# Scatter matmuls of hops 2 to 7 as four 32-column matrices instead of one of 128 columns

## The chip, the cores and the metric

The kernel runs on one core of one Trainium2 chip. The metric is the device time of one execution, in microseconds (us), as the median of several runs; lower is better. Beside the runs there is one profiled execution, whose trace gives every instruction's start and length on each engine: PE (TensorE, matmuls; PEld are its weight loads), DVE (VectorE), ACT (ScalarE), POOL (GpSimd) and SP (SyncE, which here only issues DMAs). Ends of matmuls in that trace are modelled.

## What is computed

A graph of N = 10,000 nodes with E = 160,000 random edges and D = 128 features per node. First seven propagations ("hops") of the normalized sum over neighbours, each from the result of the one before; then a small attention over the eight tokens of each node, and a readout.

```python
h = x
toks = [x]
for _ in range(7):
    msg = h[src] * deg_inv_sqrt[src, None] * deg_inv_sqrt[dst, None]
    h = _segment_sum(msg, dst, N)
    toks.append(h)
tok = jnp.stack(toks, axis=1)                      # (N, 8, D)
t = _layernorm(tok, axis=-1)
q, key, v = (einsum('nkd,de->nke', t, w) for w in (wq, wk, wv))
attn = _softmax(einsum('nkd,nld->nkl', q, key) / D ** 0.5, axis=-1)
o = tok + einsum('nkd,de->nke', einsum('nkl,nld->nkd', attn, v), wo)
alpha = _softmax(einsum('nkd,d->nk', _layernorm(o, axis=-1), w_r), axis=-1)
out = einsum('nk,nkd->nd', alpha, o)
```

## The kernel before

**Stages.** The edges are sorted into cells and turned into 0/1 matrices in fp8 (`pass_a`, `decode`, `place`, `matrices`); hop 1 runs between that work, block by block as the matrices appear. The matrices of each block of 128 target nodes are stored in DRAM (`GSd`). Hops 2 to 7 load them again and do nothing else but propagate. The attention follows. The diff touches `block`, which serves hop 1 (`first=True`) and hops 2 to 7 alike.

**A block.** The nodes stand in 79 tiles of 128. The table `tab` holds all node features in SBUF as f16 pairs (a high and a low part, 256 columns per tile). One call of `block` makes one tile of 128 targets:

- *Gather* (`gather(jj)`, L580). For each of NG = 18 groups, four 0/1 matrices of 128 x 32 pick 32 rows each out of four different table tiles. The four matmuls write the partitions 0 to 31, 32 to 63, 64 to 95 and 96 to 127 of the PSUM tile `p`. A call of `gather` makes two groups (eight matmuls), so a block calls it nine times, jj = 0 to 8. `p` rotates over 6 PSUM buffers in hops 2 to 7.
- *Evacuation* (L585, L587). The 128 x 512 result goes to an f16 buffer `e` in SBUF (14 of them in rotation): in hops 2 to 7 ACT takes jj = 0, 2, 4, 5, 7 and DVE jj = 1, 3, 6, 8. A gather that reuses a buffer of `p` waits for its evacuation six gathers earlier.
- *Scatter* (`scat(e, jj)`, L556). For each of the 18 groups one 0/1 matrix of 128 x 128 adds the 128 gathered rows into the 128 targets: a matmul of 256 columns into the PSUM accumulator `acc`, which all 18 share.
- *Rows that didn't fit* (`fetched`, L542). NI + 1 = 2 further groups per block are fetched from DRAM by POOL's indirect DMAs (`fetch`, L526, into `og`) and scattered the same way, with the matrices `w[:, NG * 128:]` and `Sov`. `begin` does so ahead of the scatters; in the first two blocks of a hop (`late`) the second of them comes in `close` (L569).
- *Close* (`close`, L571). DVE adds the high and low halves into `s`; then `entries` writes the new table entries (ACT L616, DVE L617, L618) and `token_out` the token (POOL L625, and a DMA by SP).

**Order.** Hops 2 to 7 run six times over 79 blocks. Within a block PE has all 72 gather matmuls first, then the two fetched groups, then 18 scatters. The scatters lag: `pend` holds closures, and a block leaves the last two of its own scatter calls and its `close` to the next block (`lag` = 2). So a block's 18 scatters are the last four of the block before, and fourteen of its own. POOL's queue has per block: a copy of one column of `e` of jj = 0 (L525, it holds the fetch back until that evacuation is done), the fetch from `tabh` (L526), the fetch from `tabd` (L526), and L625. SP's queue has the load of the next `w` (L752) and the stores.

Each matmul is two PE instructions, a weight load and the matmul. The names to follow: `fetched`, `scat` and `close` in `block` (L530 to L611), `gather` for comparison, and the caller in `run` (L750 to L762).

Of the kernel before, what the change touches and what calls it, by code (L numbers as in the profile page):

```python
# [20 lines left out]
NG = 18  # L21
NI = 1
# [17 lines left out]
class Hops:  # L40
# [169 lines left out]
    def times(self, out, oh, f):  # L210

        self.nc.vector.tensor_tensor(out, oh, f[:, :, None, :].to_broadcast(list(oh.shape)), op=ALU.mult)  # L212
# [317 lines left out]
    def block(self, t, w, tab, og, pend, lag, runs, first, evac, fin, lead=False, late=False, mid=None, ahead=None,  # L530
              after=None):

        nc, V, A, T, G = self.nc, self.nc.vector, self.nc.scalar, self.nc.tensor, self.nc.gpsimd
        m = 257 if first else 256
        acc = []


        def fetched(i, start=False, stop=False):  # L540
            W = w[:, (NG + i) * 128:(NG + i + 1) * 128] if i < NI else self.Sov[:, t, :]
            T.matmul(acc[0][:, :256], W, og[i], start=start, stop=stop)  # L542
            if first:
                T.matmul(acc[0][:, 256:257], W, self.ones16, start=False, stop=False)

        def begin():
            acc.append(self.pacc.tile([128, 512], F32, name="acc", tag="acc"))
            for i in range(NI if late else NI + 1):
                fetched(i, start=i == 0)

        def scat(e, jj):
            if not acc:
                acc.append(self.pacc.tile([128, 512], F32, name="acc", tag="acc"))
            for j in range(e.shape[1]):
                J = 2 * jj + j
                T.matmul(acc[0][:, :m], w[:, J * 128:(J + 1) * 128], e[:, j, :m], start=first and J == 0,  # L556
                         stop=J == NG - 1 and not (first or late))
                if first and J == 0 and not lead:
                    for i in range(NI):
                        fetched(i)  # L560

        def close():
            if first:
                if lead:
                    for i in range(NI):
                        fetched(i)
                T.matmul(acc[0][:, 256:257], self.Sov[:, t, :], self.ones16, start=False, stop=False)
            if first or late:
                T.matmul(acc[0][:, :256], self.Sov[:, t, :], og[NI], start=False, stop=True)  # L569
            s = self.fp.tile([128, 128], F32, name="s")  # L570
            V.tensor_reduce(s, acc[0][:, 0:256].rearrange("p (h d) -> p d h", h=2), axis=X, op=ALU.add)  # L571
            fin(t, s, acc[0])

        def gather(jj):
            n = min(2, NG - 2 * jj)
            p = self.pg.tile([128, 2, 2, 128], F32, name="p")
            for j in range(n):
                for q in range(4):
                    s = 4 * (2 * jj + j) + q
                    T.matmul(p[32 * q:32 * q + 32, j], w[:, NJ * 128 + s * CAP:NJ * 128 + (s + 1) * CAP], tab[:, s, :], start=True, stop=True)  # L580
            e = self.ebuf[self.eb_i % len(self.ebuf)]
            self.eb_i += 1
            pv = p[:, :n].rearrange("p j h d -> p j (h d)")
            if evac(jj):
                A.copy(e[:, :n, 0:256], pv)  # L585
            else:
                V.tensor_tensor(e[:, :n, 0:256], pv, self.one[:, :, None].to_broadcast([128, n, 256]), op=ALU.mult)  # L587
            pend.append(lambda: scat(e[:, :n], jj))

        jj = 0  # L590
        for i, n in enumerate(runs):
            for _ in range(n):
                gather(jj)
                if jj == 0 and not first and not mid:
                    ahead(self.ebuf[(self.eb_i - 1) % len(self.ebuf)][:, 0, 0:1])
                jj += 1
            if mid:
                mid(0)
            if not first:
                begin()  # L600
                if mid:
                    ahead()
            while len(pend) > lag:
                pend.pop(0)()
            if mid:
                mid(1)
            if after:
                after()
            if i == len(runs) - 1:
                pend.append(close)  # L610
            yield  # L611
# [686 lines left out]
```

## Time and profile before

| what | value |
|---|---|
| median of 3 runs | 3991.8 us (3988.98 to 3993.97) |
| the profiled execution | 3999.62 us, span 3997.8 us, mean TensorE clock 0.973 |
| PE busy | 3745.5 us (94%), 69,690 matmuls |
| PEld busy | 3031.4 us (76%) |
| DVE busy | 3322.9 us (83%) |
| ACT busy | 2724.5 us (68%) |
| POOL busy | 1766.6 us (44%) |
| chain that ended last | PE 71%, DVE 19%, ACT 4% |

Hops 2 to 7 take the stretch from about 1192 us to 3300 us of the span; the attention follows it.

How to read the lines: a group's line has the kernel's line, the engine, the operation, the tile written and the tiles read, the shape, the count, then busy time in us, the mean length of one in ns, and the idle time before them with what ended it. `128*32` on a PE line is the shape of the weights: rows by columns. A line of the timeline has start, length, engine, line and operation, merged where equal instructions follow each other (`x18`), and in brackets the idle time before and its inferred releaser; "issue" means that the profile shows nothing that was waited for. A line of the windows has the stretch, its length, busy time with the number of instructions of PE, PEld, DVE, ACT and POOL, then the granted clock of PE, the busy share of the DMA engines and GB/s.

### The profile page before, as it was taken

Reading aid. Unit: us, or ns where it says so; the run is one execution under the profiler, and the core shown is the slowest. Engines: PE = TensorE matmul, PEld = TensorE weight load, DVE = VectorE, ACT = ScalarE, POOL = GpSimd, SP = SyncE. Lnnn points to the kernel's source line nnn. Section 1 sums busy time; section 2 is a strip of 40 time slices with the busy share of each in tenths; the row PEclk is TensorE's granted clock in tenths of the full one; section 3 lists DMA queues with packets and bytes.
Section 4 is the critical chain, followed back from the end, with each engine's and each line's share of the span. In section 5 each row is a group of like instructions: output and inputs, shape, how many; then the busy total and the mean of one; then the engine's idle time right before and its main releaser. Section 6 shows DMA issues by size and latency. Waiting matters only on the chain.

```text
span 3997.8 us, 165094 instructions
## 1 busy us (share of the span) xinstructions
PE 3745.5 (94%) x69690; PEld 3031.4 (76%) x69690; DVE 3322.9 (83%) x6961; ACT 2724.5 (68%) x6830; POOL 1766.6 (44%) x2342
## 2 busy tenths in 40 slices
PE   6886799999989999999999999999999999999997
PEld 4665566666658888888888788878878887788885
DVE  8998999999977777777777777777766666999998
ACT  6884456666666666666666666666665658888884
POOL 0000333333335665666666566656656662222222
PEclk8998899999999999999999999999999999999998
DMA  3100445454556666666666666666656552222220
GB/s 104 32 2 1 134 151 154 149 162 143 156 168 189 201 201 193 202 203 200 193 202 202 185 202 202 202 189 198 202 184 205 186 183 77 74 74 76 78 78 13
DMA packets 321189, 594.93 MB, mean 149 GB/s; under 512 B 56183, under 2 KB 214101, under 8 KB 315189
## 3 DMA queue, kind: packets, MB, share of 16 engines
q1 hardware_dynamic: 282485, 506.62, 40.0%
q0 software_dynamic: 35392, 72.55, 6.3%
q8 instruction: 546, 8.95, 0.9%
q10 hardware_dynamic: 2560, 5.12, 0.4%
q14 instruction: 206, 1.69, 0.1%
HBM read 455.43 MB, written 128.67 MB: 146 GB/s over the span
## 4 chain that ended last, share of the span: by engine, by line
PE 71%; DVE 19%; ACT 4%; issue 2%; DMA 2%; POOL 0%; another core or an unknown queue 0%; SPq 0%; DVEq 0%; ACTq 0%; POOLq 0%
PE p L580 26%; PE acc L556 24%; PE acc L542 4%; DVE w L514 3%; PE pv L972 3%; PE po L983 3%; PE pu L961 3%; DVE ux L219 2%; DVE o L212 2%; ACT rs L340 2%; PE tb L440 2%; PE pt L951 1%; DVE oh L206 1%; DVE R L212 1%; DVE w L511 1%
## 5 line engine op out<-in xcount | busy, mean ns | idle before, releaser
L585 ACT CAST eb<-p 128x512 f16<-128x512 f32 x3065 | 1623.7, 596 | 645.4 <-PE p L580 404.3
L587 DVE TENSOR_TENSOR eb<-p,one 128x512 f16<-128x512 f32 x1912 | 1230.6, 685 | 332.2 <-PE acc L556 195.9
L580 PE MATMUL p<-tab,w 128*32 128x256 f16 x39816 | 1288.7, 274 | 44.2 <-issue 21.4
L556 PE MATMUL acc<-eb,w 128*128 128x256 f16 (+1 forms) x9954 | 1246.9, 274 | 8.4 <-DVE indeg L649 3.1
L580 PEld LDWEIGHTS <-w 128*32 128x32 fp8e4 x39816 | 1002.3, 96 | 261.3 <-issue 225.8
L556 PEld LDWEIGHTS <-w 128*128 128x128 fp8e4 x9954 | 954.3, 98 | 170.3 <-issue 54.9
L526 POOL DMA_INDIRECT og<-tabh,oidx x553 | 613.3, 1109 | 767.7 <-DVE vi L478 389.6
L526 POOL DMA_INDIRECT og<-tabd,oidx x541 | 586.3, 1084 | 640.2 <-PE acc L556 294.3
L625 POOL TENSOR_SCALAR r<-s,ctok 128x128 f32<-128x128 f32 x474 | 294.3, 621 | 47.7 <-DVE s L571 30.3
L616 ACT ACTIVATE tab<-s,c 128x128 f16<-128x128 f32 x395 | 158.6, 402 | 209.7 <-DVE eb L587 185.6
L617 DVE SCALAR_TENSOR_TENSOR tab<-s,c,tab 128x128 f16<-128x128 f32 x395 | 138.9, 352 | 180.8 <-issue 168.0
L571 DVE TENSOR_REDUCE s<-acc 128x128 f32<-128x256 f32 x553 | 228.7, 414 | 24.0 <-PE acc L569 11.2
L997 ACT ACTIVATE junk<-tab 128x128 f32<-128x128 f32 x625 | 245.1, 394 | 0.0
L340 ACT ACTIVATE rs<-iof,rb 128x128 fp8e4<-128x128 f32 x784 | 231.8, 389 | 0.3
L514 DVE TENSOR_TENSOR w<-dsl,iof 128x2432 fp8e4<-128x2432 f16 x79 | 211.5, 2678 | 0.0
L983 PEld LDWEIGHTS po<-v,pT 128*128 128x128 f32 x1250 | 159.5, 194 | 42.1 <-issue 27.7
L525 POOL COPY og<-eb 128x1 f16<-128x1 f16 x452 | 83.9, 186 | 241.7 <-ACT eb L585 241.7
L1055 POOL TENSOR_TENSOR p<-e,in 128x512 f32<-128x512 f32 (+1 forms) x40 | 40.8, 1020 | 321.0 <-DVE e L1053 321.0
L972 PE MATMUL pv<-Wv,xT 128*128 128x131 f32 x1250 | 176.7, 285 | 1.3 <-ACT xT L952 0.6
L983 PE MATMUL po<-v,pT 128*128 128x128 f32 x1250 | 167.0, 277 | 5.5 <-DVE tab L989 4.1
L972 PEld LDWEIGHTS pv<-Wv,xT 128*128 128x128 f32 x1250 | 154.2, 192 | 17.9 <-issue 8.8
L542 PE MATMUL acc<-og,w 128*128 128x256 f16 x553 | 156.8, 284 | 0.0
(285 smaller groups left out, 4611.9 us busy)
## 6 DMA issues: line engine op xcount, KB each, us to landing
w<-gsd SPq DMA_DIRECT2D x474, 592.0 KB
gsd<-w SPq DMA_DIRECT2D x79, 592.0 KB
rb<-srow SPq DMA_DIRECT2D x79, 576.0 KB
tok<-r SPq DMA_DIRECT2D x546, 64.0 KB
tab<-tok SPq DMA_DIRECT2D x273, 128.0 KB
tabd<-tab SPq DMA_DIRECT2D x396, 64.0 KB
og<-tabh,oidx POOLq DMA_INDIRECT x553
og<-tabd,oidx POOLq DMA_INDIRECT x541
```

The source lines that it names most:

```text
L340: A.activation(ro[:, j - a, i, :], self.iof, AF.Abs_reciprocal_sqrt, scale=2.0 ** 21, bias=rb[:, j - VP, i:i + 1], saturate=False)
L514: V.tensor_tensor(w[:, :NJ * 128].rearrange("p (j d) -> p j d", d=128), dsl[:, g, :, None].to_broadcast([128, NJ, 128]), self.iof1[:, None ...
L526: self.nc.gpsimd.indirect_dma_start(out=o, out_offset=None, in_=src[0] if i == NI else src[1], in_offset=bass.IndirectOffsetOnAxis(ap=self ...
L542: T.matmul(acc[0][:, :256], W, og[i], start=start, stop=stop)
L556: T.matmul(acc[0][:, :m], w[:, J * 128:(J + 1) * 128], e[:, j, :m], start=first and J == 0, stop=J == NG - 1 and not (first or late))
L580: T.matmul(p[32 * q:32 * q + 32, j], w[:, NJ * 128 + s * CAP:NJ * 128 + (s + 1) * CAP], tab[:, s, :], start=True, stop=True)
L585: A.copy(e[:, :n, 0:256], pv)
L587: V.tensor_tensor(e[:, :n, 0:256], pv, self.one[:, :, None].to_broadcast([128, n, 256]), op=ALU.mult)
L625: self.nc.gpsimd.tensor_scalar(r, s, ct[:, t:t + 1], None, op0=ALU.mult)
L972: T.matmul(p[:, g - a, :], S[i]["xT"][:, g, :], Wv, start=True, stop=True)
L983: T.matmul(p[:, g - a, :], PT[i % 2][:, g, :], S[i]["v"][:, g, :128], start=True, stop=True)
L997: A.activation(j, S[i]["x"][:, g, :], AF.Square, bias=S[i]["x"][:, g, 0:1], scale=-1.0, accum_out=S[i]["sq"][:, g:g + 1])
```

## The change

In hops 2 to 7 each scatter is written as four matmuls with 32 columns of the same matrix each; they read the same 256 columns of `e` (or `og`) and write the four 32-partition strips of `acc`. Which part of the sum each scatter adds, and the order of the groups, stay. Hop 1 (`first`) keeps the full matrix through the same helper.

```diff
+        def times(W, rows, start, stop):
+            if first:
+                T.matmul(acc[0][:, :rows.shape[-1]], W, rows, start=start, stop=stop)
+                return
+            for q in range(0, 128, 32):
+                T.matmul(acc[0][q:q + 32, :256], W[:, q:q + 32], rows, start=start, stop=stop, tile_position=(0, q))
 
         def fetched(i, start=False, stop=False):
             W = w[:, (NG + i) * 128:(NG + i + 1) * 128] if i < NI else self.Sov[:, t, :]
-            T.matmul(acc[0][:, :256], W, og[i], start=start, stop=stop)
+            times(W, og[i], start, stop)
...
             for j in range(e.shape[1]):
                 J = 2 * jj + j
-                T.matmul(acc[0][:, :m], w[:, J * 128:(J + 1) * 128], e[:, j, :m], start=first and J == 0,
-                         stop=J == NG - 1 and not (first or late))
+                times(w[:, J * 128:(J + 1) * 128], e[:, j, :m], first and J == 0, J == NG - 1 and not (first or late))
...
             if first or late:
-                T.matmul(acc[0][:, :256], self.Sov[:, t, :], og[NI], start=False, stop=True)
+                times(self.Sov[:, t, :], og[NI], False, True)
```

The built program has the same instructions in the same order on DVE, ACT, POOL and SP. On PE each of the 20 scatter matmuls of a block in hops 2 to 7, with its weight load, becomes four of each: 120 instructions more per block, over 6 x 79 = 474 blocks.

## The prediction

> **What bounds the kernel now.** I read the page first, then the windows of the hops, the chain of waits, and the timelines of single blocks.
>
> ```profile
> L580 PE MATMUL p<-tab,w 128*32 128x256 f16 x39816 | 1288.7, 274 | 44.2 <-issue 21.4
> L556 PE MATMUL acc<-eb,w 128*128 128x256 f16 (+1 forms) x9954 | 1246.9, 274 | 8.4 <-DVE indeg L649 3.1
> w<-gsd SPq DMA_DIRECT2D x474, 592.0 KB
> ```
>
> The x474 are the loads of `w` in hops 2 to 7, one per block: 474 blocks carry the change. A window and the chain in the middle of these hops:
>
> ```profile
> 2000.00:2200.00 200.00, 199.54 (x4213) 169.01 (x4201) 156.71 (x320) 138.90 (x274) 126.19 (x183) 1.00 0.64 202
> ```
>
> ```profile
> 2003.97 2.08 PE p L580 x72
> 2006.05 0.32 PE acc L542 x2
> 2006.37 1.97 PE acc L556 x18
> 2008.34 2.08 PE p L580 x72
> ```
>
> PE is busy 199.5 of 200 us at clock 1.00, and the chain holds nothing but PE: 72 gather matmuls, 2 fetched rows, 18 scatters, then the next block. A block takes 2008.34 - 2003.97 = 4.37 us. So a nanosecond saved on PE counts at first; the timeline of PE tells where there is one.
>
> ```profile
> 2003.90 2.15 PE L580 MATMUL p<-tab,w 128*32 128x256 f16 x72
> 2005.98 0.28 PE L542 MATMUL acc<-og,w 128*128 128x256 f16 x1
> 2006.10 0.27 PE L542 MATMUL acc<-og,Sov 128*128 128x256 f16 x1
> 2006.21 2.13 PE L556 MATMUL acc<-eb,w 128*128 128x256 f16 x18
> ...
> 2008.27 2.15 PE L580 MATMUL p<-tab,w 128*32 128x256 f16 x72
> ```
>
> 18 full scatters last 2.13 us, of which the last takes 0.27: (2.13 - 0.27)/17 = 0.109 us from one to the next. 72 gathers are 18 groups of four that stand side by side: (2.15 - 0.28)/17 = 0.110 us per group. A group of four 32-column matmuls thus costs what one full matmul costs. 38 such steps of 0.109 are 4.15 us; the block takes 4.37. The other 0.22 us lies at the two places where the shape changes: from the gathers' start, 18 steps end at 2003.90 + 1.97 = 2005.87, but L542 starts at 2005.98 (0.11 late, and the step after it is 0.12 instead of 0.109); 18 scatters end at 2006.21 + 1.97 = 2008.18, the next gather starts at 2008.27 (0.09 late, and 0.01 more on its first step). The weight loads stand idle there, for no wait that the profile knows:
>
> ```profile
> 2005.98 0.10 PEld L542 LDWEIGHTS <-w 128*128 128x128 fp8e4 x1 [0.21 <-issue]
> ...
> 2008.27 0.12 PEld L580 LDWEIGHTS <-w 128*32 128x32 fp8e4 x8 [0.21 <-issue]
> ```
>
> Is it the shape, or a wait that happens to stand there? In the attention, where a 32-column form follows a full one, the same 0.09 us appears: eight L983 at (1.05 - 0.27)/7 = 0.111 end at 3610.64, and L1003 starts at 3610.73; and on the way back a weight load sits idle 0.22 us.
>
> ```profile
> 3609.75 1.05 PE L983 MATMUL po<-v,pT 128*128 128x128 f32 x8
> 3610.73 1.30 PE L1003 MATMUL ps<-xT,uT 128*32 128x32 f32 x128
> 3612.24 0.63 PE L951 MATMUL pt<-ident,tab 128*128 128x128 f32 x4 [0.22 <-PE ps L1003]
> ```
>
> [...]
>
> **The change, part by part.** Removed: per block 20 full matmuls with their weight loads. Added: 80 of 32 columns with 80 loads, 120 more PE instructions per block, 56,880 in all. Moved: nothing; the waits stay on the first of each four, the signal on the last. By the gather's row a group takes 0.109 to 0.110, so 20 groups cost -0.00 to +0.02 us per block against the 20 full ones; I take 0.00, as both rows agree within rounding. With one shape from gather to scatter to gather, both gaps go: -0.22 us on PE. Hop 1 and the start of the attention keep theirs. If PE alone set the pace: 474 x 0.22 = 104 us.
>
> What hides behind PE is late next. The other engines around one block:
>
> ```profile
> 2008.07 0.40 ACT L616 ACTIVATE tab<-s,c 128x128 f16<-128x128 f32 x1 [0.51 <-DVE eb L587]
> 2008.50 0.35 DVE L617 SCALAR_TENSOR_TENSOR tab<-s,c,tab 128x128 f16<-128x128 f32 x1 [0.47 <-issue]
> 2008.77 0.28 DVE L618 TENSOR_REDUCE mx<-tab 128x1 f32<-128x128 f16 x1
> 2008.78 2.05 ACT L585 CAST eb<-p 128x512 f16<-128x512 f32 x4 [0.31 <-PE p L580]
> 2009.01 1.89 DVE L587 TENSOR_TENSOR eb<-p,one 128x512 f16<-128x512 f32 x3
> 2009.43 0.18 POOL L525 COPY og<-eb 128x1 f16<-128x1 f16 x1 [0.50 <-ACT eb L585]
> 2009.89 1.02 POOL L526 DMA_INDIRECT og<-tabh,oidx  x1 [0.27 <-POOL og L525]
> 2011.33 0.59 ACT L585 CAST eb<-p 128x512 f16<-128x512 f32 x1 [0.50 <-PE acc L556]
> 2011.37 0.69 DVE L587 TENSOR_TENSOR eb<-p,one 128x512 f16<-128x512 f32 x1 [0.47 <-PE acc L556]
> 2011.67 0.94 POOL L526 DMA_INDIRECT og<-tabd,oidx  x1 [0.77 <-PE acc L556]
> 2011.98 0.41 DVE L571 TENSOR_REDUCE s<-acc 128x128 f32<-128x256 f32 x1
> ...
> 2013.14 0.59 ACT L585 CAST eb<-p 128x512 f16<-128x512 f32 x1 [0.32 <-PE p L580]
> ```
>
> The fifth cast of ACT (2011.33) and the fourth copy of DVE (2011.37) read `p` of gathers that PE had started by 2010.14; yet both begin half a microsecond after their engines were free. They begin 0.42 and 0.46 us after POOL's indirect DMA ended (2009.89 + 1.02 = 2010.91). Where that DMA comes late, nothing of the sort is seen:
>
> ```profile
> 1537.61 2.48 DVE L587 TENSOR_TENSOR eb<-p,one 128x512 f16<-128x512 f32 x4
> 1539.51 1.01 POOL L526 DMA_INDIRECT og<-tabh,oidx  x1 [2.03 <-DMA tabd<-tab]
> ```
>
> There DVE's four copies run without a gap. So I read it thus: while POOL issues an indirect DMA, PE's signals reach nobody until about 0.4 us after its end. That makes a loop which PE's speed doesn't enter: ACT's first cast 2008.78, POOL's copy 2009.43 (+0.65), first DMA 2009.89 (+0.46, lasts 1.02), second DMA 2011.67 (0.76 after the first's end, lasts 0.94), and the next first cast 2013.14 (0.53 after its end). Sum 4.36 us, within 0.01 of the block. Its last link has play now: PE's first gathers of the next block end only about then. Two places show it where POOL is the later one, and the cast begins 0.58 instead of 0.51 us or more after the block's first gather:
>
> ```profile
> 1213.24 0.95 POOL L526 DMA_INDIRECT og<-tabd,oidx  x1 [0.67 <-PE acc L556]
> 1214.68 1.56 ACT L585 CAST eb<-p 128x512 f16<-128x512 f32 x3 [0.28 <-PE p L580]
> ...
> 3003.59 0.94 POOL L526 DMA_INDIRECT og<-tabd,oidx  x1 [0.88 <-PE acc L556]
> 3005.02 1.56 ACT L585 CAST eb<-p 128x512 f16<-128x512 f32 x3 [1.19 <-PE p L580]
> 3004.44 1.82 PE L580 MATMUL p<-tab,w 128*32 128x256 f16 x60
> ```
>
> Both are 0.49 us after the DMA's end. The loop is then 0.65 + 0.46 + 1.02 + 0.76 + 0.94 + 0.49 = 4.32 us; with the 0.42 of the fifth cast it is 4.25, with 0.53 it is 4.36. I take 4.32, since those two rows are of this very link.
>
> A second loop runs over DVE: fourth copy 2011.37, reduce 2011.98, ACT's L616, L617, L618 and the next block's first copy, which frees the `p` that the eighth gather wants. From 2009.01 back to the copy of the block before (2011.37 - 4.37 = 2007.00) that is 2.01, plus 0.69 for the copy itself: it is free at 2009.70, and the eighth gather starts 14 steps after 2008.27, at 2009.80: 0.1 us of play per block in which PE may move ahead, half of the gain. So this loop too, tied to POOL by the fourth copy, ends the gain somewhere around 0.1.
>
> Sum: 4.37 - 4.32 = 0.05 us per block, x 474 = 24 us. The profiled execution took 3999.6 us for a span of 3997.8; the median of the runs shown is 3991.8, 8 us less. 3999.6 - 24 = 3976 under the profiler, 3991.8 - 24 = **3968 us** for the median.
>
> Bounds of the added supply: PE's instructions per block rise from 184 to 304, from 42 to 70 per us if a block takes 4.32. The nearest rows:
>
> ```profile
> 3610.73:3611.82 1.08, 1.08 (x127) 1.08 (x128) 0.98 (x5) 1.08 (x6) 0.66 (x2) 1.00 0.00 0
> ...
> 3821.40:3827.48 6.08, 5.91 (x200) 4.96 (x199) 5.74 (x20) 5.12 (x22) 0.83 (x2) 1.00 0.17 50
> q8 instruction: 546, 8.95, 0.9%
> ```
>
> 255 instructions in 1.08 us are 235 per us: a burst is no trouble. Over some 400 the densest stretch I found has 399 in 6.08 us, 66 per us, but there the arithmetic sets the pace. Fetching is 16 KB a packet, 256 instructions, one per 3.6 us instead of 6.1. I take no cost; the far end is in the rivals.
>
> **The rivals.**
> 1. *PE alone decides* (full gain): the half microsecond is no fixed lag behind POOL but moves with PE, and both loops shrink with the block. For: the profile itself names PE's L556 as the releaser (2011.33, 2011.37, 2011.67). Against: the rows at 1537.61. Time 3991.8 - 104 = 3888.
> 2. *The loop over POOL is already tight*: its last link really is 0.53, and the 0.22 us turns into waits of the gathers for `p`. Loop 4.36, gain 0 to 0.01 per block: 3987 to 3992, no change.
> 3. *Slower, by the supply of instructions*: it decides if PE is fed fewer than 304/4.37 = 70 instructions per us over many blocks. At the 66 of the densest long stretch a block takes 304/66 = 4.61, so +0.24 x 474 = 114 us: 4105; at the 42 that the hops sustain now it would be far worse. For: no row shows more than 66 for longer than some 300 instructions. Against: nothing in that stretch waits for instructions. [...]
> 4. *The four don't stand side by side*, since they share their rows and one accumulator, unlike the gathers: 20 x 3 x 0.109 = 6.5 us more per block, over 3 ms. Against: reading the same rows and adding into the same place is what 18 full scatters do now at full rate.
>
> **How the numbers follow.** The forecast (a loop of about 4.32, gain 0.03 to 0.12 per block, 3935 to 3978) has 0.42. Rival 1 has 0.21, rival 2 0.14, rival 3 0.21, rival 4 0.02. The range goes from rival 1's price, a little widened, 3885, to 4060, where the supply would be 304/(4.37 + 68/474) = 67 per us: 0.77 and a small part of rival 3. A measurement of this kernel tells 0.2%, 8 us, from no change. Faster by more: 0.42 + 0.21 = 0.63; same: 0.14; slower: 0.23.
>
> **What would show it.** Right: no idle weight load of 0.21 us in hops 2 to 7; 20 groups of four at 0.109 us; the chain of waits now with DVE, ACT or POOL in it; gathers that wait for ACT L585 or DVE L587; a block of 4.25 to 4.34 us; POOL's two indirect DMAs at the same distance as now. Rival 1: PE still 99.8% busy, a block of 4.15. Rival 2: 4.36 with idle time on PE. Rival 3: idle "issue" on PE in the scatters, without a wait; rival 4: scatters 0.1 us apart one by one. I am wrong if PE's gaps are still there, or if a block takes over 4.37.

## The result, and the profile after

| | median | runs | ratio, 95% interval |
|---|---|---|---|
| before, beside it | 3992.2 us | 3988.98 to 3993.97, 4 runs | |
| after | 4425.8 us | 4423.21 to 4427.76, 4 runs | 1.1082, 1.1064 to 1.1099 |

The change costs 434 us: 0.92 us for each of 474 blocks. The prediction was 3968 us, with 4060 as its upper end. The profiled execution took 4426.54 us (span 4424.7, clock 0.972).

From the page of after (line numbers have moved: the gathers are L585, the scatters in fours L544):

```profile
q8 instruction: 768, 12.58, 1.2%
...
L544 PE MATMUL acc<-eb,w 128*32 128x256 f16 x34128 | 1257.4, 274 | 275.6 <-issue 267.4
L544 PEld LDWEIGHTS <-w 128*32 128x32 fp8e4 x36024 | 1003.9, 96 | 550.3 <-issue 541.4
```

Two rows are new against before. The scatters have 275.6 us of idle time ahead of them, and "issue" ended 267.4 of it: PE stood still and waited for nothing that the profile shows. And the queue that brings instructions moved 768 packets instead of 546. The 222 more are 56,880 added PE instructions in packets of 256 (56,880/222 = 256.2; 12.58 MB in 768 packets are 16.4 KB each).

The chain of waits of after (start, length, what), for the stretch that was shown of before:

```profile
2204.70 1.97 PE p L585 x72
2206.66 0.49 PE acc L544 x19
2207.15 0.26 issue
2207.41 1.59 PE acc L544 x44
2209.00 0.19 issue
2209.20 0.70 PE acc L544 x17
2209.90 1.97 PE p L585 x72
2211.87 0.59 PE acc L544 x22
2212.46 1.50 issue
```

No DVE, ACT or POOL stands in it. One block takes 2209.90 - 2204.70 = 5.20 us, the next has a hole of 1.50 us. (Measured from each of DVE's sums of `acc` to the next, the middle half of all blocks lies at 5.14 to 5.30; before, at 4.36 to 4.38.) The holes stand at places that have no wait. What does stand there shows in the timelines of PE and of POOL of after:

```profile
2204.45 2.21 PE L585 MATMUL p<-tab,w 128*32 128x256 f16 x72
2206.42 0.35 PE L544 MATMUL acc<-og,w 128*32 128x256 f16 x4
2206.53 0.35 PE L544 MATMUL acc<-og,Sov 128*32 128x256 f16 x4
2206.64 0.51 PE L544 MATMUL acc<-eb,w 128*32 128x256 f16 x11
2207.41 1.59 PE L544 MATMUL acc<-eb,w 128*32 128x256 f16 x44 [0.26 <-issue]
2209.20 0.70 PE L544 MATMUL acc<-eb,w 128*32 128x256 f16 x17 [0.19 <-issue]
```

```profile
2206.11 1.02 POOL L526 DMA_INDIRECT og<-tabh,oidx  x1 [0.27 <-POOL og L525]
2207.89 0.94 POOL L526 DMA_INDIRECT og<-tabd,oidx  x1 [0.75 <-PE acc L544]
```

The first fetched group follows the gathers without a gap: 2204.45 + 18 x 0.109 = 2206.41 (2206.42 in the row). Groups of four follow each other at 0.11 (2206.42, 2206.53, 2206.64). But PE goes on only 0.28 us after the end of POOL's first indirect DMA (2206.11 + 1.02 = 2207.13; 2207.41), and 0.37 after that of the second (2208.83; 2209.20). The hole at 2212.46 is of another kind (it is explained with e1). So there were two suspects, tried one by one.

### The profile page after: what moved, and what is told of

The parts are those of the page before. It is cut to its first block, busy times and chain, and to the rows that moved or that the text cites. A ratio compares the mean times of both kernels' runs of the same rounds, so it can differ in the third digit from the quotient of the medians.

```text
span 4424.7 us, 221970 instructions
## 1 busy us (share of the span) xinstructions
PE 3861.7 (87%) x98130; PEld 3203.9 (72%) x98130; DVE 3343.1 (76%) x6961; ACT 2723.8 (62%) x6830; POOL 1766.2 (40%) x2342
## 3 DMA queue, kind: packets, MB, share of 16 engines
q8 instruction: 768, 12.58, 1.2%
## 4 chain that ended last, share of the span: by engine, by line
PE 68%; DVE 18%; issue 9%; ACT 2%; DMA 1%; SPq 0%; DVEq 0%; POOL 0%; ACTq 0%; POOLq 0%
PE acc L544 28%; PE p L585 23%; DVE w L514 3%; PE pv L977 3%; PE po L988 3%; PE pu L966 2%; DVE ux L219 2%; DVE o L212 2%; PE acc L541 2%; PE tb L440 1%; PE pt L956 1%; DVE oh L206 1%; DVE R L212 1%; DVE w L511 1%; DVE ohp L206 1%
## 5 line engine op out<-in xcount | busy, mean ns | idle before, releaser
L544 PE MATMUL acc<-eb,w 128*32 128x256 f16 x34128 | 1257.4, 274 | 275.6 <-issue 267.4
L544 PEld LDWEIGHTS <-w 128*32 128x32 fp8e4 x36024 | 1003.9, 96 | 550.3 <-issue 541.4
L585 PE MATMUL p<-tab,w 128*32 128x256 f16 x39816 | 1318.2, 274 | 43.7 <-issue 19.5
L585 PEld LDWEIGHTS <-w 128*32 128x32 fp8e4 x39816 | 1087.2, 97 | 147.8 <-issue 119.5
L525 POOL COPY og<-eb 128x1 f16<-128x1 f16 x452 | 83.0, 184 | 599.4 <-ACT eb L590 599.3
L541 PE MATMUL acc<-eb,w 128*128 128x257 f16 x1422 | 232.9, 279 | 7.8 <-DVE indeg L654 2.4
L544 PE MATMUL acc<-og,Sov 128*32 128x256 f16 x1848 | 161.2, 273 | 24.5 <-issue 24.5
L544 PE MATMUL acc<-og,w 128*32 128x256 f16 x1896 | 162.8, 273 | 13.8 <-issue 13.8
L541 PEld LDWEIGHTS <-w 128*128 128x128 fp8e4 x1501 | 119.7, 98 | 74.8 <-issue 57.8
```

Source lines behind the costliest of these rows:

```text
L541: T.matmul(acc[0][:, :rows.shape[-1]], W, rows, start=start, stop=stop)
L544: T.matmul(acc[0][q:q + 32, :256], W[:, q:q + 32], rows, start=start, stop=stop, tile_position=(0, q))
```

## The experiments

Two words are used below. *Supply*: PE's instructions come in packets of 256, and fewer arrive than the change needs (56.5 per us in the result, counted below, against 304/4.15 = 73). *Hold*: while POOL issues an indirect DMA, PE is cut off (in the rows above it goes on 0.28 and 0.37 us after the DMA's end). The kernel before, which ran beside every group, took 3992 to 3996 us on some chips and 3941 to 3942 on others. The traces tell the two kinds apart: POOL's second indirect DMA follows the first by 0.75 us, as in the rows above, or by 0.30, as here in d3, which is the changed kernel on a chip of the second kind:

```profile
2206.12 1.02 POOL L526 DMA_INDIRECT og<-tabh,oidx  x1 [0.27 <-POOL og L525]
2207.44 0.94 POOL L526 DMA_INDIRECT og<-tabd,oidx  x1 [0.30 <-PE acc L544]
```

I call the first kind holding chips. Each group ran on one chip, and no chip in two groups, so it may as well be something else that lasts as long as a group. What it is stays open.

**Group 1, a holding chip (the kernel before: 3993.3).** POOL's two indirect DMAs per block, in hops 2 to 7, become plain DMAs of fixed rows on SP, without the copy L525: in the changed kernel (e1) and in the kernel before (e2). In e3 this is done in the changed kernel for `tabd` alone, and the copy stays. In e6 each indirect DMA is split into two of 64 rows.

The edit of e1 and e2 in `fetch`; e3 has `if self.plain and i == NI:`.

```diff
+        if self.plain:
+            self.nc.sync.dma_start(o, (src[0] if i == NI else src[1])[0:128, :])
+            return o
```

That of e6:

```diff
-        self.nc.gpsimd.indirect_dma_start(out=o, out_offset=None, in_=src[0] if i == NI else src[1],
-                                          in_offset=bass.IndirectOffsetOnAxis(ap=self.oidx[:, t, i:i + 1], axis=0))
+        n = 64 if self.plain else 128
+        for r in range(0, 128, n):
+            ix = self.oidxb[r // n] if r else self.oidx
+            self.nc.gpsimd.indirect_dma_start(out=o[r:r + n], out_offset=None, in_=src[0] if i == NI else src[1],
+                                              in_offset=bass.IndirectOffsetOnAxis(ap=ix[:n, t, i:i + 1], axis=0))
```

> The changed kernel, but in hops 2 to 7 the two row fetches of a block are plain DMAs of 128 fixed rows from SP's queue in place of POOL's indirect ones (wrong rows are fetched, the copy ahead of the first fetch is left out). Theory A (while POOL issues an indirect DMA, PE is not fed with instructions until some 0.3 us after its end, and what PE holds in advance covers 1 us of full scatters but not of 32-column ones): the stalls go, a block takes 4.15 to 4.25 us, 3880 to 3930 us in all. Theory B (the fetch of PE's own instructions from memory is too slow for 304 per block, whatever POOL does): the stalls stay, a block 5.1 to 5.3 us, 4350 to 4430 us. Theory C (scatters of four are slow in themselves): 4350 to 4430 us.

> The kernel before with the same plain DMAs in place of POOL's indirect ones. Theory A: PE was covered before, so a block stays at 4.37 us and the time at 3960 to 3995 us; but PE's signals are no longer held back, so DVE's four evacuations of a block run without the gap of half a microsecond. If that gap belongs to PE's change of shape and not to POOL, it stays. Theory B: the same time, nothing said of the gap.

> The changed kernel with only the second of the two fetches (that from tabd) as a plain DMA from SP; the first stays on POOL. Theory A: about half of the stalls: a block of 4.6 to 4.8 us, 4100 to 4200 us. Theory B: 4350 to 4430 us.

> The changed kernel with each indirect fetch of hops 2 to 7 split into two of 64 rows; everything is computed. Theory A: if an indirect DMA of 64 rows takes POOL about half as long (0.5 to 0.6 us), each hold is short enough to be covered by what PE has in advance, and the time falls to 3900 to 4050 us; if it takes nearly the 1 us of 128 rows, there are four holds per block and the time rises to 4700 to 4950 us. Theory B: 4350 to 4430 us, no change by POOL.

| kernel | median | ratio, 95% interval |
|---|---|---|
| e1, fours, no POOL DMA | 4341.3 us | 1.0867, 1.0836 to 1.0898 |
| e2, full matrices, no POOL DMA | 3945.0 | 0.9877, 0.9860 to 0.9894 |
| e3, fours, one POOL DMA | 4294.2 | 1.0754, 1.0731 to 1.0777 |
| e6, fours, four POOL DMAs of 64 rows | 5957.2 | 1.4918, 1.4883 to 1.4953 |

None of the four fell into a range that had been expected: e1 lies 9 us below theory B's, e2 15 us below theory A's, e3 between the two, and e6 far above. But without any POOL DMA the change still costs 348 us, so the hold alone isn't the cause. PE's timeline in e1 shows what is left:

```profile
2202.42 1.60 PE L548 MATMUL acc<-eb,w 128*32 128x256 f16 x50 [1.17 <-issue]
2203.75 2.23 PE L589 MATMUL p<-tab,w 128*32 128x256 f16 x72
2205.72 0.38 PE L548 MATMUL acc<-og,w 128*32 128x256 f16 x4
2205.82 0.28 PE L548 MATMUL acc<-og,Sov 128*32 128x256 f16 x2
2206.99 0.29 PE L548 MATMUL acc<-og,Sov 128*32 128x256 f16 x2 [0.89 <-issue]
2207.00 2.25 PE L548 MATMUL acc<-eb,w 128*32 128x256 f16 x72
2208.97 1.70 PE L589 MATMUL p<-tab,w 128*32 128x256 f16 x54
2211.01 0.72 PE L589 MATMUL p<-tab,w 128*32 128x256 f16 x18 [0.34 <-issue]
```

Count the matmuls from one stall to the next: 50 + 72 + 4 + 2 = 128, then 2 + 72 + 54 = 128. Each is two instructions, so PE stops after 256, in the middle of a group of four or of the gathers, wherever that falls. (Not after every 256: some packets come in time. But of the 173 stalls over 0.1 us that e1 has from 1400 to 2600 us, 172 stand at this place in the count.) The trace's records of the instruction queue agree: a packet starts at 2204.67, takes 1.08 us, and PE goes on at 2206.99, 2.3 us after the packet's start; the next starts at 2208.13, and PE goes on at 2211.01. Only one packet is under way at a time: in no trace here does one start before the last has landed (none of the 768 of the result does). The hole at 2212.46 in the result is such a stop. It stands at the same place in the count, a packet starts at 2211.52, and PE goes on at 2213.96. Few instructions are there in advance: in the traces of the result, e1, e8, c3, d1 and d3 no packet starts more than 289 instructions before PE needs it.

e2 shows the hold by itself: it takes the kernel before to 3945, close to the time that it has on the other chips, and DVE's four copies now run without the gap (0.47 us ahead of the fourth) that the prediction had put down to POOL:

```profile
2204.12 2.48 DVE L591 TENSOR_TENSOR eb<-p,one 128x512 f16<-128x512 f32 x4 [0.54 <-PE p L584]
```

The block in the middle of a hop stays at 4.37 us in e2; the 48 us lie at the ends of the hops and ahead of hop 2. e3 lies 47 us below e1 although it keeps one of the two holds; the plain DMAs seem to cost something themselves, as group 4 shows again. e6 shows how dear the hold gets. A DMA of 64 rows keeps POOL nearly as long as one of 128 (0.91 to 0.97 us against 0.94 to 1.02), four of them follow each other, and in each pause PE gets a handful of matmuls done. POOL's and PE's timelines in e6:

```profile
2201.15 0.97 POOL L530 DMA_INDIRECT og<-tabh,oidx  x1 [0.51 <-POOL og L526]
2202.42 0.91 POOL L530 DMA_INDIRECT og<-tabh,oidxb  x1 [0.30 <-issue]
```

```profile
2202.46 0.32 PE L548 MATMUL acc<-eb,w 128*32 128x256 f16 x4 [0.19 <-issue]
2203.19 0.40 PE L548 MATMUL acc<-eb,w 128*32 128x256 f16 x6 [0.40 <-issue]
```

Not all of e6's time is the hold: the clock granted to PE from 1900 to 2250 us was 0.88, against 0.99 in the result.

**Group 2, a chip that doesn't hold (the kernel before: 3941.4).** Fours for some of the scatters only, which sets the instructions per block: 244 (e7_four_in_10: the two fetched groups and jj = 7, 8, 0, 1) and 280 (e7_four_in_16: those and jj = 2, 3, 4). e8 is the changed kernel with the matrices `w` of four blocks loaded once and used in turn. e9 is the kernel before without four of the 18 scatters.

The edit of e7_four_in_10, and of e7_four_in_16 with `jj in (7, 8, 0, 1, 2, 3, 4)`:

```diff
-        def times(W, rows, start, stop):
-            if first:
+        def times(W, rows, start, stop, four=True):
+            if first or not four:
...
-                times(w[:, J * 128:(J + 1) * 128], e[:, j, :m], first and J == 0, J == NG - 1 and not (first or late))
+                times(w[:, J * 128:(J + 1) * 128], e[:, j, :m], first and J == 0, J == NG - 1 and not (first or late), jj in (7, 8, 0, 1))
```

That of e8:

```diff
-                    w = self.gsp.tile([128, (NJ + NG) * 128], F8, name="w")
-                    nc.sync.dma_start(w, self.GSd[t])
+                    if k == 2 and n < 4:
+                        w = self.gsp.tile([128, (NJ + NG) * 128], F8, name=f"wk{n}", bufs=1)
+                        nc.sync.dma_start(w, self.GSd[t])
+                        kept.append(w)
+                    w = kept[n % len(kept)]
```

And of e9, against the kernel before:

```diff
+                if not first and j and jj in (2, 3, 4, 5):
+                    continue
```

> The changed kernel with four matrices only in those 10 groups of a block that PE meets first after the gathers (the two fetched ones and the scatter calls jj = 7, 8, 0, 1); the other 10 are one matrix of 128 as before, so both changes of shape stay. PE has 244 instructions per block. Theory B (PE's instructions come in pieces of 256 and at no more than some 57 per us over long stretches): 244/57 = 4.28 us is still under the 4.37 of the kernel before, so 3980 to 4060 us. Theory C (a scatter of four costs more in itself): half of the loss and no gain, 4200 to 4300 us.

> The same with four matrices in 16 of the 20 groups: 280 PE instructions per block, both changes of shape stay. Theory B: 280/57 = 4.9 us per block, 4200 to 4260 us: the loss begins only where the instructions per block pass some 250 (57 x 4.37). Theory C: in proportion to the groups, 4350 to 4450 us.

> The changed kernel, but the matrices of only four blocks are loaded, once, and used for all blocks of hops 2 to 7 (wrong sums): the 592 KB per block from DRAM fall away. Theory B1 (a piece of instructions takes its 2.3 us whatever else the DMA engines do): 4380 to 4430 us. Theory B2 (the pieces stand behind the loads of the matrices): the stalls shrink, under 4200 us.

> The kernel before without four of the 18 scatters of a block in hops 2 to 7 (the second of the two in jj = 2 to 5; wrong sums): PE alone would need 34 x 0.109 + 0.22 = 3.93 us per block. It tests the step of the prediction that a loop over POOL's two indirect DMAs holds a block at about 4.32 us however fast PE is. By that step 3968 us (3935 to 3992). If PE alone decides: 474 x 0.44 less, 3785 us.

| kernel | PE instructions per block | median | ratio, 95% interval |
|---|---|---|---|
| e7_four_in_10 | 244 | 3954.1 us | 1.0025, 1.0012 to 1.0037 |
| e7_four_in_16 | 280 | 4106.9 | 1.0417, 1.0396 to 1.0439 |
| e8_four_no_w_loads | 304 | 4017.3 | 1.0195, 1.0175 to 1.0216 |
| e9_one_14_scatters | 176 | 3743.2 | 0.9500, 0.9481 to 0.9519 |

60 more instructions per block cost 13 us, 36 beyond those cost 153 us: a limit that sets in between 244 and 280, and no price per instruction. Both lie below theory B's ranges (by 26 and 93 us), which were worked out with the rate of a holding chip. Loads of `w` matter: without them the change costs 76 us, and 279 with them (d3 in group 4). In e9 a block takes 2207.04 - 2203.11 = 3.93 us, so all that the four scatters had cost (4 x 0.109) is saved; the chain of waits of e9:

```profile
2203.11 2.08 PE p L582 x72
2207.04 2.08 PE p L582 x72
```

But e8 and e9 had run on a chip of the other kind than the result. So both were run again.

**Group 3, a holding chip (the kernel before: 3996.4).** The changed kernel, the kernel before, e8 and e9 once more, as c1 to c4.

> The changed kernel again, beside c3, which differs from it in the loads of w alone. Two cases, told apart by the kernel before in this group and by the gap between POOL's two indirect DMAs in the traces: 0.76 us and 3992 us for the kernel before (POOL's DMAs hold PE's signals), or 0.30 us and 3941 us (they don't). Theory 'supply' (PE's instructions arrive in pieces of 256, some 57 per us beside the loads of w): 4426 in the first case; in the second 4285 to 4345, as in e1 and e3, where the hold was taken away in another way. Rival 'hold' (the 434 us come mostly from POOL's hold): in the second case under 4050.

> The kernel before, for its trace beside the others of this group. No difference between it and the runs beside it: ratio 1.000 within 0.003. Where its time is near 3941 both theories expect 0.30 us from the end of POOL's first indirect DMA to its second and DVE's four copies without a gap; where it is near 3992, 0.76 us and a gap of about half a microsecond ahead of the fourth.

> The change, with the matrices of four blocks loaded once and used in turn. Theory 'supply': pieces land sooner when the DMA engines are free, 64 to 67 instructions per us instead of 57: 0.55 to 0.75 us per block less than c1, so 4070 to 4165 where c1 is 4426, about 4017 where c1 is 4285 to 4345. Rival 'the loads don't matter': within 0.5% of c1.

> The kernel before without 4 of the 18 scatters of each block (0.44 us of PE less per block). 'PE alone': 3.93 us per block, 198 to 207 us less than the kernel before. 'Loop over POOL' (the prediction's, 4.32 us, which exists only where POOL's DMAs hold PE's signals): 4.3 us per block, no more than 50 us less than the kernel before, where that takes 3992; where it takes 3941 there is no such loop and it is 198 us less, as before.

| kernel | median | ratio, 95% interval |
|---|---|---|
| c1_after | 4444.6 us | 1.1107, 1.1085 to 1.1129 |
| c2_before | 3996.3 | 0.9998, 0.9987 to 1.0010 |
| c3_four_no_w_loads | 4370.7 | 1.0930, 1.0910 to 1.0950 |
| c4_one_14_scatters | 3888.3 | 0.9722, 0.9702 to 0.9742 |

c3 missed both expectations. What took 4017 on the other chip takes 4371 here, with the loads gone in both. PE and POOL in the timeline of c3:

```profile
2203.37 2.23 PE L585 MATMUL p<-tab,wk 128*32 128x256 f16 x72
...
2205.05 1.02 POOL L526 DMA_INDIRECT og<-tabh,oidx  x1 [0.27 <-POOL og L525]
...
2205.57 0.60 PE L544 MATMUL acc<-eb,wk 128*32 128x256 f16 x13
...
2206.36 1.40 PE L544 MATMUL acc<-eb,wk 128*32 128x256 f16 x43 [0.18 <-issue]
...
2206.80 0.95 POOL L526 DMA_INDIRECT og<-tabd,oidx  x1 [0.74 <-PE acc L544]
...
2208.13 0.66 PE L544 MATMUL acc<-eb,wk 128*32 128x256 f16 x16 [0.37 <-issue]
...
2208.56 2.19 PE L585 MATMUL p<-tab,wk 128*32 128x256 f16 x72
```

This block repeats with hardly a change: 2208.56 - 2203.37 = 5.19 us. Both stalls end 0.3 to 0.4 us after the end of a DMA of POOL (2206.07 and 2206.36, 2207.75 and 2208.13), and nothing is waited for. Over 216 first DMAs of this trace with a stall, PE starts 59 to 62 more instructions after the DMA's start and then is dry, 0.87 us after it. (After the second DMA it is mostly 47 to 51, 0.68 us after the start; PE had been dry half a microsecond earlier. In the result it is mostly 54 to 61 after the first.) e8, the same kernel on a chip that doesn't hold, has next to no late starts of this kind (3 us in all, in the table after group 4). So I read it thus: POOL's DMA cuts off not only PE's signals, as the prediction had read, but also its instructions, and PE lives on some 60 that it has. The kernel before issues only 2/0.109 = 18 instructions per us in its scatters, so 60 would last 3.3 us there and outlast the 1.3 us from a DMA's start until PE goes on; the changed kernel issues 8/0.109 = 73 per us all the time.

c4 lies between its two expectations: 108 us less than before, not 200 and not 50. On a holding chip there is a loop that e9, on the other chip, doesn't have; it is discussed below.

**Group 4, a chip that doesn't hold (the kernel before: 3942.3).** d1 has both changes of e1 and of e8, d2 is e7_four_in_10, d3 the changed kernel, d4 is e1.

> The change with both suspects taken away at once in hops 2 to 7: no indirect DMA by POOL (as e1) and no loads of w but four (as e8). Two theories of where the 430 us of the change come from. 'Either is enough': POOL's DMAs starve PE (c3: about 1.0 us per block) and the loads of w delay the pieces of instructions (e1: about 0.7), and they cover each other when both are there; then this is the only one of the four cells without a large loss, 3970 to 4040. Rival 'only one of them counts, the chips differ': it stays within 1.5% of c3, 4305 to 4435, or within 1.5% of e1, 4275 to 4405.

> Ten groups of four per block, those right behind the gathers, and ten full scatters. Theory 'some 60 instructions' (while POOL issues an indirect DMA, and 0.3 to 0.4 us longer, PE gets no new instructions and lives on about 60 that it has): the block's first DMA falls into 32-column work at 73 per us, which is dry after 0.87 us and loses about 0.45 us; the second falls into full scatters at 18 per us and loses nothing. 4.37 + 0.45 = 4.8 us per block, 3996 + 0.3 to 0.45 x 474 = 4140 to 4210, where the kernel before takes 3996; 1.0025 of it as in e7 where it takes 3941. Rival 'the hold only delays signals': under 1.01 of the kernel before in both cases.

> The changed kernel beside d1, d2 and d4. Where the kernel before takes about 3996: 4426 to 4445. Where it takes about 3941, so that POOL's DMAs hold nothing, 'either is enough' expects what e1 has: 4285 to 4345.

> e1 again, beside d1 (which differs from it in the loads of w alone) and d3 (which has POOL's DMAs). Both theories: 4325 to 4355, whatever the chip does with POOL's DMAs, as there are none in hops 2 to 7; stalls at every 256th PE instruction and nowhere else.

| kernel | median | ratio, 95% interval |
|---|---|---|
| d1_four_neither | 3985.0 us | 1.0107, 1.0090 to 1.0124 |
| d2_four_in_10 | 3953.6 | 1.0027, 1.0017 to 1.0037 |
| d3_after | 4220.8 | 1.0692, 1.0669 to 1.0715 |
| d4_four_no_pool_dma | 4360.1 | 1.1065, 1.1046 to 1.1083 |

d1 comes out as "either is enough" had it. d4 is 5 us over its range. d3 is 64 us under its own, and d4 139 us above d3: the plain DMAs of e1 and d4 seem to be themselves a load that the indirect ones aren't, so e1 overstates what the loads of `w` do alone. That e1 (4341) and d4 (4360) are close on chips of the two kinds fits: with no DMA by POOL there is nothing to hold.

d1 also shows what the change would bring if instructions came in time. PE's timeline in d1:

```profile
2204.23 2.23 PE L589 MATMUL p<-tab,wk 128*32 128x256 f16 x72
2206.20 0.38 PE L548 MATMUL acc<-og,wk 128*32 128x256 f16 x4
2206.31 0.38 PE L548 MATMUL acc<-og,Sov 128*32 128x256 f16 x4
2206.41 2.23 PE L548 MATMUL acc<-eb,wk 128*32 128x256 f16 x72
2208.38 2.46 PE L589 MATMUL p<-tab,wk 128*32 128x256 f16 x72
```

2208.38 - 2204.23 = 4.15 us: the block without its two changes of shape, as predicted. Only some blocks come through so: in the middle half of them a block takes 4.27 to 4.67.

The traces can also be asked where the time is lost. I took, from 1400 to 2600 us, every matmul that starts more than 0.16 us after the one before it, less the usual 0.109, and counted apart those that stand at the packets' place (6 of each 128 places in the count of matmuls):

| trace | lost at the packets' place, us | lost elsewhere, us |
|---|---|---|
| e1: loads of `w`, plain DMAs, no hold | 243 | 8 |
| d3: loads of `w`, no hold | 185 | 8 |
| e8: no loads of `w`, no hold | 95 | 3 |
| d1: no loads of `w`, plain DMAs, no hold | 76 | 4 |
| c3: no loads of `w`, hold | 9 | 213 |
| result: loads of `w`, hold | 96 | 144 |

The 9 of c3 are chance (20 of its 542 late starts). So supply and hold are two things, and the result has both. The traces also show what the loads of `w` do to the supply. A packet takes about 1 us in all of these, but its start comes later: from the matmul at which PE would stop for one packet to the start of the next packet it is a median of 1.2 us in e8 and 1.5 in d1, against 1.9 in d3 and 2.6 in e1. Why the start waits, no trace shows.

**Group 5 (the kernel before: 3941.2; again a chip that doesn't hold).** f1 is e7_four_in_10 once more, f2 has its ten groups of four at the end of a block (`jj in (2, 3, 4, 5, 6)`) instead of behind the gathers.

> The kernel of d2: ten groups of four per block, the ten right behind the gathers. Where the kernel before takes about 3996 (POOL's DMAs hold PE's signals). Theory 'some 60 instructions': the first indirect DMA falls into 32-column work and costs 0.3 to 0.45 us per block, the second falls into full scatters and costs nothing: 4140 to 4210. Rival 'late signals only': under 1.01 of the kernel before, 4036. Where the kernel before takes about 3941: 3954 by both.

> The same number of instructions as f1 (244 per block), but the ten groups of four are the last ten of a block, right ahead of the next gathers. Where the kernel before takes about 3996. Theory 'some 60 instructions': the first DMA meets the end of the gathers and full scatters (about 30 + 18 instructions) and costs nothing, the second starts in the groups of four, PE is dry some 0.65 us later and loses 0.4 to 0.65 us: 4180 to 4305, its stalls behind POOL's second DMA where those of f1 are behind the first. Rival 'late signals only': as f1, under 4036. Where the kernel before takes about 3941: within 1% of f1 by both.

| kernel | median | ratio, 95% interval |
|---|---|---|
| f1_first_10 | 3950.1 us | 1.0026, 1.0016 to 1.0036 |
| f2_last_10 | 3963.3 | 1.0063, 1.0046 to 1.0080 |

Both theories expected this here, so the two say nothing of the hold: whether the place of the dense stretch decides on a holding chip hasn't been seen. They do show that a change of shape is not got rid of by using fours for half the scatters, but moved into the scatters. PE's timeline in f1:

```profile
2207.38 1.04 PE L544 MATMUL acc<-eb,w 128*32 128x256 f16 x32
2208.35 1.27 PE L541 MATMUL acc<-eb,w 128*128 128x256 f16 x10
2209.55 2.15 PE L585 MATMUL p<-tab,w 128*32 128x256 f16 x72
```

Eight groups from 2207.38 end at 2208.25, the full ones begin at 2208.35. No version that computes the same was found to beat the kernel before.

## Why the prediction was wrong

**The step that failed: "I take no cost" for the supply.** The prediction put the price of 120 more PE instructions per block at nothing and kept 24 us of gain; the supply alone cost some 380 us by the table below. A second cost, that PE itself is starved while POOL issues a DMA, had no term in the prediction at all: 155 us. A window inside hops 2 to 7, with PE's and PEld's instructions in brackets, in the result, in d3 and in d1 in turn:

```profile
1900.00:2250.00 350.00, 305.06 (x9893) 265.55 (x9885) 226.59 (x466) 196.06 (x389) 178.34 (x256) 0.99 0.55 166
```

```profile
1900.00:2250.00 350.00, 306.29 (x10623) 285.01 (x10615) 243.32 (x501) 207.83 (x420) 192.87 (x276) 1.00 0.60 179
```

```profile
1900.00:2250.00 350.00, 337.64 (x11875) 310.14 (x11871) 268.40 (x559) 231.39 (x470) 47.00 (x78) 1.00 0.23 64
```

That is (9893 + 9885)/350 = 56.5 instructions per us, 60.7 and 67.8; e8, counted in the same way, has 66.2. The prediction had the right threshold, 70, and a block at its full gain needs 304/4.15 = 73. Even with both suspects gone PE gets 68: one packet of 256 every 3.76 us (319 packets in 1200 us of d1). The prediction's "one per 3.6 us instead of 6.1" was thus more than this queue gave over such a stretch in any run, though half of d1's packets follow within 3.51 us, the time in which PE at full rate uses one up (256/73). With about one packet ahead (289 instructions at most), a late one stops PE, and nothing makes up for it. Its row of 255 instructions in 1.08 us was no evidence: that is about one packet, and the last packet before it had started 11 us earlier, so that they lay ready. And the 399 in 6.08 us were kept down by arithmetic (PE was busy for 5.91 of them), so they bounded the supply from below only, while the prediction used them as the likely far end.

Rival 3 named the mechanism and its sign, idle "issue" in the scatters without a wait; it had 0.21. Its price, 4105, was taken at 66 per us, which only kernels without the loads of `w` reach, and it left out the hold. (From the first gather of hop 2 to the last sum the 474 blocks took 2556 us, 5.39 each, after 2132 us, 4.50 each, before. That 304/56.5 = 5.38 agrees is no confirmation, as the 56.5 was counted in the same trace.)

**Where the 434 us come from.** One order in which the parts add up, from the medians:

| step | us |
|---|---|
| the two changes of shape gone, 474 x 0.22 (worked out from the blocks of 4.15 in d1) | -104 |
| supply without the loads of `w` and without POOL's DMAs (d1 against 3942.3 - 104) | +147 |
| POOL's own fetches instead of plain ones (e8 against d1, each from its own before) | +33 |
| loads of `w` (d3 against e8, each from its own before) | +203 |
| hold (the result's +434 against d3's +279) | +155 |
| sum | 434 |

The first two lines are one measurement, d1's +43, split by a sum. The last two cover each other. Where the hold is there, taking the loads away brings only 4444.6 - 4370.7 = 74 us. Where the loads are away, the hold costs 374 - 76 = 298 us (c3 and e8, each from its own before). That a PE which stands still for the one gives the next packet time to come for the other is a likely reason, and the table after group 4 fits it: 96 us at the packets' place in the result, 185 in d3. The step of 33 is small and between chips, and not certain in its cause.

**The other steps.**
- *PE bounds the block at 4.37*: right. Without four scatters it is 3.93 where nothing holds (e9).
- *Four stand side by side at the price of one, and both changes of shape go*: right, -0.22 us per block, the blocks of 4.15 in d1. Rival 4 is out: groups follow at 0.11.
- *POOL cuts off PE's signals until about 0.4 us after its DMA*: borne out by e2 on a holding chip for the first DMA, and absent on the others, where the second DMA follows by 0.30 us and not 0.75. What the prediction didn't ask is what else is cut off.
- *A loop over POOL of 4.32 us that leaves 0.05 of the gain*: mis-sized. In c4, where PE alone would take 3.93, half of the blocks take over 4.23, a tenth over 4.32 and a quarter under 3.94. These rows of POOL, DVE and ACT in the timeline of c4 show one:

```profile
2419.68 1.02 POOL L526 DMA_INDIRECT og<-tabh,oidx  x1 [0.27 <-POOL og L525]
...
2421.08 0.69 DVE L589 TENSOR_TENSOR eb<-p,one 128x512 f16<-128x512 f32 x1 [0.37 <-PE acc L558]
...
2421.39 0.95 POOL L526 DMA_INDIRECT og<-tabd,oidx  x1 [0.69 <-DMA tabd<-tab]
...
2422.48 2.05 ACT L587 CAST eb<-p 128x512 f16<-128x512 f32 x4
```

  DVE's fourth copy does begin 0.38 us after the first DMA's end (2420.70). But the next first cast begins 0.14 after the second's (2422.34), not 0.49: that link isn't there. The chain of waits of c4 runs through DVE in this block (2421.09 to 2423.74) and names POOL nowhere. Which link sets 4.23 wasn't settled.

If instructions had come in time, the gain on a holding chip would, by the median of c4, have been some 0.14 per block, between the forecast and rival 1; that is argued, no run had both.

## What to carry to other kernels

A split that costs an engine no time may still cost it instructions. Count them per block, divide by the block's time, and compare with a rate that some kernel has sustained over several instruction packets, not with a burst of one packet: here between 56 and 68 PE instructions per us for the changed kernel, by what else the DMA engines and POOL do (35 in e6). A stall that the profile calls "issue" without a wait was read here by its place: at multiples of 256 instructions (172 of 173 stalls in e1) it was the packet, 0.3 to 0.4 us behind the end of a DMA issued by POOL the hold.

## What was not expected of the hardware

- Packets of 256 PE instructions came one at a time: in the result none of 768 starts before the last has landed. Where PE stopped for one, it went on 2.2 to 3.0 us after the packet's start (e1, d3, e8, d1), though the packet itself took about 1 us.
- On some chips POOL's indirect DMA left PE with some 60 instructions (59 to 62 in c3) until 0.3 to 0.4 us after its end; on others nothing of this was seen (away from the packets' place 3 us were lost in e8, 213 in c3). For the kernel before that is 3992 to 3996 against 3941 to 3942 us, 1.3%: runs on different chips aren't compared here without the kernel before beside each.
- An indirect DMA of 64 rows kept POOL 0.91 to 0.97 us (e6), one of 128 rows 0.94 to 1.02 (the result).
